# Reordered loads, a four-bank second layer for block 0 and moved weight sums in a retention and feed-forward kernel

## The chip, the core and the metric

The kernel runs on one core of one Trainium2 chip. The metric is the device time of one execution, in microseconds (us). Five engines matter, each with an instruction queue of its own that is worked off in order: PE (TensorE, the matrix multiplications), DVE (VectorE), ACT (ScalarE), POOL (GpSimd) and SP (SyncE, which here only issues DMA transfers). Matmul results land in PSUM, which holds eight banks of 128 x 512 fp32; everything else lives in SBUF.

## The reference

For each of 8 batches and 8 heads, 576 tokens of 64 dimensions go through retention (attention without a softmax, with a decay per head); the result, 4608 tokens of 512 values, goes through a two-layer network with GELU.

```python
scores = scale * q @ k.T                         # per batch and head
ret = scores * Dmat                              # Dmat[i, j] = gamma_h ** (i - j) for i >= j, else 0
x = (ret @ v) -> (4608, 512)                     # heads side by side
h = x @ w_in                                     # 512 -> 2048
out = (0.5 * h * (1 + tanh(c * (h + 0.044715 * h**3)))) @ w_out   # 2048 -> 512
```

All inputs and the output are fp32; the kernel computes in fp16 with fp32 sums.

## The kernel before, in words

**Blocks.** The network works on nine blocks of 512 tokens, t = 0 to 8. Block t below 8 holds the first 512 tokens of batch t; block 8 holds the last 64 tokens of all batches. While PE computes block t, the retention of batch t + 1 is woven in between. Batch 1 is thus prepared during block 0, batch 2 during block 1.

**Retention of batches 0 to 2.** The 512 tokens go in two groups g of 256 tokens. A group's inputs are six load tiles of 128 x 512 fp32 (256 KB): two each of q, k and v (`load`, L91). Each is cast to fp16 (`cast`, L244), q and k with a decay factor. Then, in this order: `turn` (L275) transposes q and k on PE, eight 128 x 128 transposes into one bank `tr`, and one engine copies them to `tt` in SBUF; `state2` (L341) multiplies k by v into two banks `us`; `score2` (L313) makes the scores in banks `st`, two for each half x; `masks2` (L327) multiplies them by the causal mask into `ret` on DVE and frees the bank; `scan` (L405, DVE) carries the decayed state on and frees `us`, and `spread` (L419, ACT) writes it as fp16; `past` and `av2` (L425, L356) make the output `xs`, and `put` (L455, ACT) copies that to `xT`.

**The network.** First layer: `up_half` (L480) does eight matmuls of 256 columns into a bank `hp` for half a block, and ACT applies GELU from `hp` into `gT`. Second layer of block 0: `down_mm` (L504), plain matmuls of 512 columns into a bank `op[i]` for each of four groups of 128 tokens, summed over 16 tiles of w_out; `store_pair` (L509) copies two banks to `ost` and stores them. Second layer of blocks 1 to 8: a seven-product scheme (`prod`, `after`, L548 and L568) in place of eight products. It needs sums of quarters of w_out, `wt` 1 to 4 (`weight_sums`, L525: four DVE instructions of 128 x 1024 fp16 for half of the rows; the call with f = 4 needs the last eight w_out tiles of the order below), and sums of quarters of gT (`act_sums`, L536: four DVE instructions).

**Loads.** `seq` (L124 to L131) lists all load tiles in the order in which SP issues them: batch 0, the 16 w_in tiles, the 16 w_out tiles in the order FO (L125), then batch by batch. They go through a ring of LD = 16 buffers; `pump` (L134) issues the next load when a cast has freed a buffer. w_out tiles are cast by POOL and DVE in turn (`cast_w`, L622, and WENG, L634).

**Order of the work.** The order on each engine is written out by hand. Each block is a list of PE steps, its *units* (L839 on); `at(t, u, f)` (L703) puts the work f behind unit u of block t. Block 0 has here 16 units of first layer before unit 0 (numbered -16 to -1) and 34 units of second layer (L842): for the banks op[0] and op[1] 16 units of two `down_mm` each and a store, then the same for op[2] and op[3]. Block 1 has 16 units of `up_half` (0 to 15) and 14 of `prod`, two for each product (products 1, 6, 5, 7, 2, 4, 3 at units 16 to 29). `group` (L718) places the two transposes, a first part (state, scores, masks) and a second part (past, av, put) of a group, `casts2` (L746) its casts. "(0, 17)" below is unit 17 of block 0.

PSUM banks are handed out in the order in which they were given back (`bank`, `drop`, L61 and L67): a matmul into a new bank waits until the bank's last reader is done.

Of the kernel before, what the change touches and what calls it, by code (L numbers as in the profile page):

```python
# [20 lines left out]
def kernel(  # L21
# [97 lines left out]
    def body(b):  # L119
        if b < NPE:  # L120
            return [("b", b, key, 2 * g + y) for g in range(2) for key in "qkv" for y in range(2)]
        return [("b", b, key, c) for c in range(NC) for key in "kqv"]

    seq = body(0) + [("i", g, ct) for g in range(4) for ct in range(4)]  # L124
    FO = [f + g for f in (0, 4) for g in (0, 1, 2, 3, 8, 9, 10, 11)]  # L125
    seq += [("o", f) for f in FO]
    TP = {2: 0, 4: 2, 6: 4, 7: 6}
    for b in range(1, B):
        seq += body(b)
        if b - 1 in TP:  # L130
            seq.append(("t", TP[b - 1]))  # L131
    q_ld = {"next": 0, "free": LD, "hold": False}
# [96 lines left out]
    def new_casts(b):  # L229
        a = att[b]  # L230
        for key in "kqv":
            a[key] = sb.tile([128, W], F16, tag="c" + key, name="c" + key, bufs=1 if key == "q" else 2)
# [38 lines left out]
    def new_turned(b):  # L271
        att[b]["tt"] = t = sb.tile([128, 2, NB, 128], F16, tag="tt", name="tt", bufs=2)
        att[b]["tk"], att[b]["tq"] = t[:, 0], t[:, 1]

    def turn(b, g, key, copies):  # L275
        a = att[b]
        n = HP // len(copies)
        src = a[key][:, 1024 * g : 1024 * g + 1024].rearrange("p (i j x) -> p i j x", j=2, x=2 * D)
        dst = a["tt"][:, "kq".index(key), 8 * g : 8 * g + 8, :]
        for x, cp in enumerate(copies):  # L280
            full = bank("tr", F16)
            t = full[:, 0 : 256 * n].rearrange("p (i j t) -> p i j t", j=2, t=128)
            for i in range(n):
                for j in range(2):
                    nc.tensor.transpose(t[:, i, j], src[:, n * x + i, j], ident)  # L285
            o = dst[:, 2 * n * x : 2 * n * x + 2 * n]
            if key == "q":
                o = o.rearrange("p (i h) (t j) -> p i j (h t)", h=2, j=2)
            else:
                o = o.rearrange("p (i j) t -> p i j t", j=2)  # L290
            cp(out=o, in_=t)
            drop(full)
# [20 lines left out]
    def score2(b, g, xs=(0, 1)):  # L313
        a = att[b]
        for x in xs:
            st = [bank("st") for _ in range(2)]
            for p in (2 * x, 2 * x + 1):
                for j in range(2):
                    o = 256 * (p % 2) + 128 * j
                    for h, hl in TILES:  # L320
                        nc.tensor.matmul(
                            st[hl][hv(h), o : o + 128], a["tt"][hv(hl), 0, 8 * g + 2 * p + j, hv(h)],
                            tq(b, 2 * g + h, p)[hv(hl)], start=True, stop=True,
                        )
            a["st", g, x] = st

    def masks2(b, g, x):  # L327
        for hl, t in enumerate(att[b].pop(("st", g, x))):
            r = sb.tile([128, 512], F16, tag="ret", name="ret", bufs=6)
            nc.vector.tensor_tensor(  # L330
                out=r.rearrange("p (n i) -> p n i", n=2), in0=t.rearrange("p (n i) -> p n i", n=2),
                in1=pm.rearrange("p j i -> p (j i)").unsqueeze(1).to_broadcast([128, 2, 256]), op=ALU.mult,
            )
            drop(t)
            att[b]["ret"][g, hl, x] = r
# [83 lines left out]
    def spread(b, c, cp):  # L419
        w = att[b].pop(("w", c))  # L420
        for hl in range(2):
            r = slice(64 * hl, 64 * hl + 64)
            cp(out=(tbd[b % 2][r, c, :, r] if c < NC - 1 else tbt[b % NT4][r, :, r]), in_=w[r])  # L423
# [98 lines left out]
    W11, W12 = w_out_sb[:, 0:NH, 0:HD], w_out_sb[:, 0:NH, HD:DM]  # L522
    W21, W22 = w_out_sb[:, NH:NF, 0:HD], w_out_sb[:, NH:NF, HD:DM]

    def weight_sums(f, ns=range(4)):  # L525
        s = slice(f, f + 4)
        for n in ns:
            o, x, y, f = (
                ("1", W12, W11, ALU.subtract), ("3", W22, W12, ALU.subtract),
                ("2", wt["3"], W11, ALU.add), ("4", W21, wt["2"], ALU.subtract),  # L530
            )[n]
            nc.vector.tensor_tensor(out=wt[o][:, s], in0=x[:, s], in1=y[:, s], op=f)  # L532

    gs = {}

# [86 lines left out]
    def cast_w(kind, *i):  # L622
        src = w_raw.pop((kind,) + i)
        if kind == "i":
            g, ct = i
            dst = w_in_sb[:, ct, 512 * g : 512 * g + 512]
        else:
            dst = w_out_sb[:, i[0], :]
        eng = WENG[kind][CP[kind] % len(WENG[kind])]
        CP[kind] += 1  # L630
        eng(out=dst, in_=src)  # L631
        pump(1)
# [13 lines left out]
    def later(b, c):  # L646
        scan(b, c)
        spread(b, c, A.copy)
# [54 lines left out]
    def at(t, u, f, last=False):  # L703
        events.setdefault((t, u, last), []).append(f)
# [5 lines left out]

    at(0, -12, lambda: [V.memset(x, 0.0) for x in (tbd[1][:, 1:], *tbt[1:])])
    for n, f in enumerate(FO):
        at(0, -5 + n // 4, lambda f=f: cast_w("o", f))
        if n > 8 and n % 2:
            at(0, -5 + n // 4, lambda n=n: weight_sums(0, [(n - 9) // 2]))


    def group(b, g, turns, s, o, own=True, ahead=()):  # L718
        for w, key, cp in zip(turns, "qk", (A.copy if b == 1 else T, A.copy)):
            at(*w, lambda key=key, cp=cp: turn(b, g, key, (cp,)))  # L720

        def first():
            if own:
                state2(b, g)
            score2(b, g)
            if own:
                later(b, 2 * g)
            masks2(b, g, 0)
            if own:
                masks2(b, g, 1)  # L730
                scan(b, 2 * g + 1)
            else:
                at(s[0], s[1] + 1, lambda: masks2(b, g, 1))

        def second():
            past(b, 2 * g), past(b, 2 * g + 1), av2(b, g)
            for x in ahead:
                state2(*x)
            put(b, 2 * g), put(b, 2 * g + 1)

        at(*s, first)
        at(*o, second)
        if own:
            at(o[0], o[1] + 1, lambda: spread(b, 2 * g + 1, A.copy))

    def casts2(b, g, kq, v, e):  # L746
        at(*kq, lambda: [cc(b, key, 2 * g + y, P) for key in "qk" for y in range(2)])
        at(*v, lambda: [cc(b, "v", 2 * g + y, e) for y in range(2)])

    at(0, 6, lambda: (new_casts(1), new_turned(1)))  # L750
    casts2(1, 0, (0, 7), (0, 21), A)
    group(1, 0, ((0, 17), (0, 20)), (0, 23), (0, 30))
    casts2(1, 1, (0, 14), (0, 29), A)
    at(0, 28, lambda: weight_sums(4))
    group(1, 1, ((0, 27), (0, 31)), (1, 1), (1, 6))
    at(1, 0, lambda: (new_casts(2), new_turned(2)))
    casts2(2, 0, (1, 0), (1, 0), P)
    group(2, 0, ((1, 4), (1, 7)), (1, 11), (1, 16), ahead=((2, 1),))
    casts2(2, 1, (1, 4), (1, 4), P)
    at(1, 17, lambda: later(2, 2))  # L760
    at(1, 23, lambda: later(2, 3))
    group(2, 1, ((1, 10), (1, 13)), (1, 20), (1, 26), own=False)
    at(1, 8, chunk_masks)

    at(6, 0, lambda: load_tails(TP[7]))
    at(6, 18, lambda: cast_tails(TP[7]))
# [72 lines left out]
    for t in range(NTB):  # L839
        steps = []  # L840
        if t == 0:
            for i0 in (0, 2):  # L842
                for f in FO:
                    steps.append(lambda f=f, i0=i0: [down_mm(0, i0 + n, f) for n in range(2)] and None)
                steps.append(lambda i0=i0: store_pair(0, i0, (A.copy, V.tensor_copy)))
        else:
            for u in range(2 if t == 1 else 0):
                for f in (0, NH, 2, NH + 2, 4, NH + 4, 6, NH + 6):
                    def half(u=u, f=f):
                        up_half(t, u, f)  # L850
                        if f in (NH + 2, NH + 6):
                            return lambda: act_sums(t, f - NH - 2, f - NH + 2, slice(u, u + 1))
                    steps.append(half)
            for f in range(0 if t == 1 else NH):
                steps.append(lambda f=f: up(t, f))
                def hi(f=f):
                    up(t, f + NH)
                    if f % 2:
                        return lambda: act_sums(t, f - 1, f + 1)
                steps.append(hi)  # L860
            for m in (1, 6, 5, 7, 2, 3, 4) if t == NTB - 1 else (1, 6, 5, 7, 2, 4, 3):
                for u in range(2):
                    steps.append(lambda m=m, u=u: (prod(t, m, u), after(t, m, u)))
        for u, s in enumerate(steps):
            then = s()
            run(t, u)
            if callable(then):
                then()
            run(t, u, True)
# [31 lines left out]
```

## Time and profile before

| | us |
|---|---|
| median of 3 runs | 300.15 (298.98 to 300.69) |
| the profiled execution, whole | 300.83 |
| its span (first to last instruction) | 298.9 |
| PE busy in the span | 284.7 |
| PE busy in 0 to 34 us | 27.41 of 34.00 |
| PE busy in 34 to 58 us | 20.99 of 24.00 |
| PE busy in 58 to 290 us | 232.00 of 232.00 |
| PE busy in 290 us to the end | 4.32 of 8.90 |

The last four rows are busy times of PE in stretches of the span. Second-layer matmuls of block 0 begin at 33.86 us, first-layer matmuls of block 1 at 53.99 us, products of block 1 at 74.04 us. "Busy" of PE runs to the modelled end of a matmul. An idle time is put down to the instruction or transfer that released it last.

### The profile page before, as it was taken

The numbers are of one execution on the slowest core, as the hardware profiler recorded it, in microseconds if no ns is written. First come the engines' busy times: TensorE is split into PE (matmuls) and PEld (weight loads), VectorE is DVE, ScalarE is ACT, GpSimd is POOL, SyncE is SP. The second block draws the span as 40 slices with busy tenths as digits, with TensorE's granted clock in tenths as the row PEclk, the third lists the DMA queues.
The fourth block names the chain that finished last, engine by engine and source line by source line (L and its number), as shares of the span: only waits on it lengthen the run. The fifth ranks groups of instructions, "written<-read, shape, count | busy, mean of one in ns | idle before, by whom it ended". The sixth has DMA issues, their size and how long they took to land.

```text
span 298.9 us, 7301 instructions
## 1 busy us (share of the span) xinstructions
PE 284.7 (95%) x3028; PEld 197.2 (66%) x3028; DVE 171.9 (58%) x353; ACT 163.4 (55%) x302; POOL 98.8 (33%) x129
## 2 busy tenths in 40 slices
PE   6779988899999999999999999999999999999993
PEld 2458645688884488448844885488548854884582
DVE  6790445998754874476548654855486535233432
ACT  5377426788438673766376736664665356307500
POOL 4677377970790074006700650058030000000000
PEclk9999999999999999999999999999999999999998
DMA  7999999999889999999999959944931030012004
GB/s 200 309 352 350 371 271 293 246 289 211 178 147 230 227 217 183 268 207 195 118 245 227 181 99 263 219 90 86 255 86 37 2 140 0 2 50 94 0 0 140
DMA packets 129057, 52.89 MB, mean 177 GB/s; under 512 B 101633, under 2 KB 120577, under 8 KB 129025
## 3 DMA queue, kind: packets, MB, share of 16 engines
q1 hardware_dynamic: 128544, 51.92, 73.7%
q10 hardware_dynamic: 480, 0.52, 0.6%
q8 instruction: 23, 0.38, 0.5%
q14 instruction: 10, 0.07, 0.1%
HBM read 36.70 MB, written 9.44 MB: 154 GB/s over the span
## 4 chain that ended last, share of the span: by engine, by line
PE 80%; DMA 10%; DVE 4%; SPq 3%; POOL 2%; ACT 1%; issue 0%; DVEq 0%; POOLq 0%
PE hp L469 33%; PE opB L561 14%; PE opA L561 10%; PE opC L561 10%; PE hp L487 4%; DMA ld<-in_moe_w_out_dram 4%; SPq L96 2%; PE xs L448 2%; PE st L372 2%; DMA ld<-in_moe_w_in_dram 2%; DMA ld<-in_q_dram 2%; DMA ld<-in_v_dram 2%; DVE wt L532 2%; PE xs L439 1%; PE us L397 1%; PE tr L285 1%
## 5 line engine op out<-in xcount | busy, mean ns | idle before, releaser
L469 PE MATMUL hp<-xT,w_in_sb 128*128 128x512 f16 x448 | 98.9, 380 | 0.0
L475 ACT ACTIVATE gT<-hp 128x512 f16<-128x512 f32 x112 | 64.9, 597 | 45.3 <-PE hp L469 44.8
L469 PEld LDWEIGHTS <-w_in_sb 128*128 128x128 f16 x448 | 43.3, 98 | 50.6
L561 PEld LDWEIGHTS <-gT 128*128 128x128 f16 x512 | 49.0, 98 | 7.1 <-issue 0.7
L561 PEld LDWEIGHTS <-s 128*128 128x128 f16 x384 | 37.0, 98 | 4.9
L543 DVE TENSOR_TENSOR s<-gT 128x512 f16<-128x512 f16 x32 | 14.0, 436 | 44.4 <-ACT gT L475 44.4
L827 POOL COPY gate<-s 128x1 f16<-128x1 f16 x5 | 0.9, 189 | 92.3 <-DVE s L546 92.3
L561 PE MATMUL opB<-wt,gT 128*128 128x256 f16 x256 | 30.9, 273 | 0.5 <-DVE ost L575 0.5
L487 PE MATMUL hp<-xT,w_in_sb 128*128 128x256 f16 x256 | 30.2, 273 | 1.1 <-POOL w_in_sb L631 1.0
L561 PE MATMUL opA<-w_out_sb,gT 128*128 128x256 f16 x256 | 30.8, 273 | 0.0
L487 PEld LDWEIGHTS <-w_in_sb 128*128 128x128 f16 x256 | 24.4, 98 | 5.1 <-POOL w_in_sb L631 1.6
L423 ACT CAST tbd<-ws 64x256 f16<-64x256 f32 x48 | 19.3, 403 | 15.3 <-DVE ws L414 13.6
L381 DVE TENSOR_TENSOR ret<-st,cm 128x512 f16<-128x512 f32 x40 | 24.8, 681 | 0.0
L575 DVE TENSOR_TENSOR k<-k,opB 128x512 f32<-128x512 f32 x16 | 11.0, 687 | 22.2 <-PE opB L561 16.3
L605 ACT COPY ost<-opA 128x512 f32<-128x512 f32 x8 | 4.7, 586 | 34.2 <-PE opA L561 19.9
L264 POOL TENSOR_TENSOR cq<-ld,sc 128x512 f16<-128x512 f32 x20 | 21.9, 1095 | 0.0
L493 ACT ACTIVATE gT<-hp 128x512 f16<-128x512 f32 x32 | 18.5, 600 | 5.3 <-PE hp L487 5.0
L458 ACT CAST xT<-xs 128x512 f16<-128x512 f32 x36 | 19.3, 592 | 3.3 <-PE xs L362 1.9
L264 POOL TENSOR_TENSOR ck<-ld,sc 128x512 f16<-128x512 f32 x20 | 20.8, 1040 | 0.0
L414 DVE TENSOR_TENSOR ws<-vs,gt 128x256 f32<-128x256 f32 x24 | 16.0, 669 | 1.2
L575 DVE TENSOR_TENSOR ost<-k,opC 128x512 f32<-128x512 f32 x16 | 11.0, 687 | 9.8 <-PE opC L561 9.5
L575 DVE TENSOR_TENSOR ost<-k,opB 128x512 f32<-128x512 f32 (+1 forms) x9 | 5.7, 629 | 18.7 <-PE opB L561 18.7
(93 smaller groups left out, 359.1 us busy)
## 6 DMA issues: line engine op xcount, KB each, us to landing
ld<-in_q_dram SPq DMA_DIRECT2D x32, 256.0 KB, 5.4
ld<-in_k_dram SPq DMA_DIRECT2D x32, 256.0 KB, 5.3
ld<-in_v_dram SPq DMA_DIRECT2D x32, 256.0 KB, 5.3
out_dram<-ost SPq DMA_DIRECT2D x16, 512.0 KB, 3.5
ld<-in_moe_w_in_dram SPq DMA_DIRECT2D x16, 256.0 KB, 6.2
ld<-in_moe_w_out_dram SPq DMA_DIRECT2D x16, 256.0 KB, 6.1
lt<-in_k_dram SPq DMA_DIRECT2D x8, 128.0 KB, 5.1
lt<-in_q_dram SPq DMA_DIRECT2D x8, 128.0 KB, 4.4
```

The lines of the kernel that those rows point to most:

```text
L264: eng.tensor_tensor(out=dst.rearrange("p (h d) -> p h d", d=D), in0=raw.rearrange("p (h d) -> p h d", d=D), in1=sc[:, s0].unsqueeze(2).to_ ...
L381: nc.vector.tensor_tensor(out=r.rearrange("p (n i) -> p n i", i=128), in0=t.rearrange("p (n i) -> p n i", i=128), in1=(cm if b < PAIR else ...
L414: nc.vector.tensor_tensor(out=w, in0=uc, in1=gt, op=ALU.mult)
L423: cp(out=(tbd[b % 2][r, c, :, r] if c < NC - 1 else tbt[b % NT4][r, :, r]), in_=w[r])
L458: nc.scalar.copy(out=xT[:, g0 : g0 + 2], in_=xs.rearrange("p (n g t) -> p g n t", n=HP, g=2))
L469: nc.tensor.matmul(hp.rearrange("p (g t) -> p g t", t=TL), w_in_sb[:, ct, 128 * fc : 128 * fc + 128], xT[:, o : o + TB // TL, ct, :], star ...
L475: nc.scalar.activation(out=gT[t][:, fc].rearrange("p i n -> p (i n)"), in_=hp, func=AF.Gelu_apprx_tanh)
L487: nc.tensor.matmul(hp[:, 256 * x : 256 * x + 256].rearrange("p (g t) -> p g t", t=TL), w_in_sb[:, ct, 128 * (f + x) : 128 * (f + x) + 128] ...
L493: nc.scalar.activation(out=gT[t][:, f : f + 2, 2 * u : 2 * u + 2, :].rearrange("p f i n -> p f (i n)"), in_=hp.rearrange("p (f n) -> p f n ...
L543: nc.vector.tensor_tensor(out=s["1"], in0=a21, in1=a22, op=ALU.add)
L561: nc.tensor.matmul(op[tag][:, HD * u : HD * u + HD], lhs(f), rhs[:, f], start=(new and u == 0 and f == 0), stop=(f == NH - 1), skip_group_ ...
L575: nc.vector.tensor_tensor(out=o, in0=a, in1=b, op=ALU.add)
```

## The change

Six edits:

1. `seq` lists the first six tiles of batch 1 (group 0: q, k, v) behind the twelfth w_out tile; the last four w_out tiles follow, then the rest of batch 1.
2. Block 0's second layer runs in two turns over all four banks: the first twelve w_out tiles for op[0] and op[1] (units 0 to 11), then for op[2] and op[3] (12 to 23), then the last four tiles for each pair (24 to 27, store at 28; 29 to 32, store at 33). Four banks are held from unit 12 on.
3. The last four w_out tiles are cast by POOL alone, behind unit 6. The first four weight sums (f = 0) move to unit -3; the other four (f = 4), which lay together at (0, 28), go in pairs to (1, 9) and (1, 12).
4. With four banks held, group 0 of batch 1 takes its scores in two halves of two banks each, units 20 and 24 (`apart=4`). Its spread of the second state goes to (1, 1).
5. The casts, transposes and parts of batch 1 and 2 move: casts of q and k of batch 1 from units 7 and 14 to 2 and 14, v from ACT at units 21 and 29 to ACT at 18 and POOL at 15; transposes of group 0 from units 17 and 20 to 13 and 17, of group 1 from 27 and 31 to 31 and (1, 0); the first part of group 0 from unit 23 to 20, that of group 1 stays at (1, 1). In batch 2 some events move by one unit. The chunk masks go from (1, 8) to (1, 14).
6. The transposed q of batch 2 is copied by ACT in place of DVE; of the second store of block 0, both copies are on DVE.

```diff
@@ load order @@
-    seq += [("o", f) for f in FO]
+    LATE = 12
+    seq += [("o", f) for f in FO[:LATE]]
     TP = {2: 0, 4: 2, 6: 4, 7: 6}
+    seq += body(1)[:6] + [("o", f) for f in FO[LATE:]] + body(1)[6:]
     for b in range(1, B):
-        seq += body(b)
+        seq += body(b) if b > 1 else []
@@ cast_w @@
-        eng = WENG[kind][CP[kind] % len(WENG[kind])]
+        eng = WENG[kind][CP[kind] % len(WENG[kind])] if CP[kind] < LATE or kind == "i" else nc.gpsimd.tensor_copy
@@ events @@
     for n, f in enumerate(FO):
-        at(0, -5 + n // 4, lambda f=f: cast_w("o", f))
-        if n > 8 and n % 2:
-            at(0, -5 + n // 4, lambda n=n: weight_sums(0, [(n - 9) // 2]))
+        at(0, -5 + n // 4 if n < LATE else 6, lambda f=f: cast_w("o", f))
+        if 8 <= n < LATE:
+            at(0, -5 + n // 4, lambda n=n: weight_sums(0, [n - 8], V))
@@ group @@
-        for w, key, cp in zip(turns, "qk", (A.copy if b == 1 else T, A.copy)):
-            at(*w, lambda key=key, cp=cp: turn(b, g, key, (cp,)))
+        for w, key in zip(turns, "qk"):
+            at(*w, lambda key=key: turn(b, g, key, (A.copy,)))
 ...
-            score2(b, g)
+            score2(b, g, (0,) if apart else (0, 1))
             if own:
                 later(b, 2 * g)
             masks2(b, g, 0)
+            if own and not apart:
+                masks2(b, g, 1)
             if own:
-                masks2(b, g, 1)
                 scan(b, 2 * g + 1)
-            else:
+            if apart:
+                at(s[0], s[1] + apart, lambda: (score2(b, g, (1,)), masks2(b, g, 1)))
+            elif not own:
                 at(s[0], s[1] + 1, lambda: masks2(b, g, 1))
@@ placing @@
-    at(0, 6, lambda: (new_casts(1), new_turned(1)))
-    casts2(1, 0, (0, 7), (0, 21), A)
-    group(1, 0, ((0, 17), (0, 20)), (0, 23), (0, 30))
-    casts2(1, 1, (0, 14), (0, 29), A)
-    at(0, 28, lambda: weight_sums(4))
-    group(1, 1, ((0, 27), (0, 31)), (1, 1), (1, 6))
+    at(0, -1, lambda: (new_casts(1), new_turned(1)))
+    casts2(1, 0, (0, 2), (0, 18), A)
+    group(1, 0, ((0, 13), (0, 17)), (0, 20), (0, 29), apart=4, late=(1, 1))
+    casts2(1, 1, (0, 14), (0, 15), P)
+    group(1, 1, ((0, 31), (1, 0)), (1, 1), (1, 5), late=(1, 6))
     at(1, 0, lambda: (new_casts(2), new_turned(2)))
     casts2(2, 0, (1, 0), (1, 0), P)
-    group(2, 0, ((1, 4), (1, 7)), (1, 11), (1, 16), ahead=((2, 1),))
+    group(2, 0, ((1, 4), (1, 6)), (1, 10), (1, 15), ahead=((2, 1),))
     casts2(2, 1, (1, 4), (1, 4), P)
-    at(1, 17, lambda: later(2, 2))
+    at(1, 9, lambda: weight_sums(4, (1, 2), V))
+    at(1, 12, lambda: weight_sums(4, (0, 3), V))
+    at(1, 16, lambda: later(2, 2))
     at(1, 23, lambda: later(2, 3))
-    group(2, 1, ((1, 10), (1, 13)), (1, 20), (1, 26), own=False)
-    at(1, 8, chunk_masks)
+    group(2, 1, ((1, 9), (1, 12)), (1, 20), (1, 26), own=False)
+    at(1, 14, chunk_masks)
@@ units of block 0 @@
-            for i0 in (0, 2):
-                for f in FO:
+            for i0, fs in ((0, FO[:LATE]), (2, FO[:LATE]), (0, FO[LATE:]), (2, FO[LATE:])):
+                for f in fs:
                     steps.append(lambda f=f, i0=i0: [down_mm(0, i0 + n, f) for n in range(2)] and None)
-                steps.append(lambda i0=i0: store_pair(0, i0, (A.copy, V.tensor_copy)))
+                if fs[-1] == FO[-1]:
+                    steps.append(lambda i0=i0: store_pair(0, i0, (V.tensor_copy if i0 else A.copy, V.tensor_copy)))
```

More of the change, by code (lines that the diff above doesn't have):

```diff
@@ L523, with weight_sums @@
     W21, W22 = w_out_sb[:, NH:NF, 0:HD], w_out_sb[:, NH:NF, HD:DM]
-    def weight_sums(f, ns=range(4)):
+    def weight_sums(f, ns, eng):
         s = slice(f, f + 4)
@@ L531, in weight_sums @@
             )[n]
-            nc.vector.tensor_tensor(out=wt[o][:, s], in0=x[:, s], in1=y[:, s], op=f)
+            eng.tensor_tensor(out=wt[o][:, s], in0=x[:, s], in1=y[:, s], op=f)
     gs = {}
@@ L712, with group @@
     for n, f in enumerate(FO):
-        at(0, -5 + n // 4, lambda f=f: cast_w("o", f))
-        if n > 8 and n % 2:
-            at(0, -5 + n // 4, lambda n=n: weight_sums(0, [(n - 9) // 2]))
-    def group(b, g, turns, s, o, own=True, ahead=()):
-        for w, key, cp in zip(turns, "qk", (A.copy if b == 1 else T, A.copy)):
-            at(*w, lambda key=key, cp=cp: turn(b, g, key, (cp,)))
+        at(0, -5 + n // 4 if n < LATE else 6, lambda f=f: cast_w("o", f))
+        if 8 <= n < LATE:
+            at(0, -5 + n // 4, lambda n=n: weight_sums(0, [n - 8], V))
+    def group(b, g, turns, s, o, own=True, ahead=(), apart=0, late=None):
+        for w, key in zip(turns, "qk"):
+            at(*w, lambda key=key: turn(b, g, key, (A.copy,)))
         def first():
@@ L743, in group @@
         if own:
-            at(o[0], o[1] + 1, lambda: spread(b, 2 * g + 1, A.copy))
+            at(*(late or (o[0], o[1] + 1)), lambda: spread(b, 2 * g + 1, A.copy))
     def casts2(b, g, kq, v, e):
```

## The prediction

> **What bounds the kernel now.** I read the page's busy shares first, then PE's busy time by stretches, then what PE waited for, then the chain of waits in the stretch with gaps.
>
> The page: span, shares, and PE's row of the 40 slices (tenths busy, 7.5 us each).
>
> ```profile
> span 298.9 us, 7301 instructions
> PE 284.7 (95%) x3028; PEld 197.2 (66%) x3028; DVE 171.9 (58%) x353; ACT 163.4 (55%) x302; POOL 98.8 (33%) x129
> PE   6779988899999999999999999999999999999993
> ```
>
> PE is the bound, and its gaps lie in the start, in slices 5 to 8 and at the end. The change touches nothing ahead of 33 us and nothing of the last block. It adds and removes no PE instruction: both programs have 6058 PE rows in the order of instructions. So it can only gain PE's gaps between 34 us and the point from which PE is full; the table of stretches above has 232.00 of 232.00 us busy from 58 to 290 us. The stretches between (us, busy us and instructions of PE, PEld, DVE, ACT, POOL, then clock, DMA share, GB/s):
>
> ```profile
> 34.00:54.00 20.00, 18.07 (x198) 9.34 (x196) 11.23 (x19) 8.93 (x14) 13.77 (x15) 1.00 1.04 291
> 54.00:74.00 20.00, 18.93 (x328) 16.56 (x328) 18.53 (x31) 15.54 (x29) 11.03 (x15) 1.00 1.00 249
> ```
>
> The prize is 1.93 + 1.07 = 3.00 us, 1.0% of the time, and no more. PE's waits from 33.8 to 60 us (total, times, longest):
>
> ```profile
> PE st L321 <- DVE ost L513: 1.1, 1, 1.1
> PE tr L285 <- POOL cq L256: 1.0, 1, 1.0
> PE us L348 <- ACT cv L251: 0.8, 2, 0.4
> ```
>
> Three gaps, then: 1.02 us until batch 1's q is cast (in PE's timeline the transposes at 42.39 us), 0.78 us until its v is cast (0.45 and 0.33, at 46.76 and 47.28 us), 1.07 us until a bank is free for scores (57.62 us). 0.13 us is in crumbs. Why they arise stands in the chain of waits (start, duration):
>
> ```profile
> 34.63 5.48 DMA ld<-in_q_dram
> ...
> 40.28 2.05 POOL cq L256 x2
> 42.33 2.02 POOL ck L256 x2
> ...
> 52.00 2.07 DVE wt L532 x2
> ...
> 54.09 1.43 DVE wt L532
> ...
> 55.54 1.42 DVE wt L532
> 56.96 0.61 DVE ost L513
> ...
> 57.62 0.41 PE st L321 x15
> ```
>
> Gap one is the transfer: q is issued behind 16 w_out tiles and lands at 40.1 us. Gap three is the four weight sums at (0, 28): 5.0 us on DVE with the copy that frees the op bank queued behind them.
>
> **Part 1, the earlier loads (edit 1).** The transfers run back to back, so order decides. DVE's timeline starts the cast of the twelfth w_out tile at 36.57 us, on its landing. In the casts that wait for w_out a tile takes 0.67 us (DVE at 28.57, POOL at 29.27, DVE at 29.91); from q's landing at 40.1 to the third q tile, whose cast starts at 45.20, six tiles pass, 0.84 each. So batch 1's first tile lands at 36.55 + 0.85 = 37.4, the four q and k tiles by 39.9, v by 41.6, the late w_out tiles at 42.3 to 44.3, and the third q tile at 45.15 as before, since the bytes ahead of it are the same. POOL has just finished its sixth w_out cast (35.95, 0.79 us) and casts q and k in 4 x 1.02: q ready at 39.5, k at 41.5.
>
> PE's side: a unit is 0.435 us (eight matmuls from 48.10 to 49.84). From 33.86, unit 13 ends at 39.95, the q transposes take 0.45 (42.39 to 42.84), unit 17 ends at 42.1, the k transposes at 42.6, unit 20 at 43.9. q is 0.45 us ahead of its use, k 0.6. **Gap one goes: -1.02**, and with it the crumbs, -0.13. The late w_out tiles, cast by POOL (0.61 to 0.8 each) by 45.0, are wanted at unit 24, about 47 us. Those casts stand ahead of group 1's q, k and v casts in POOL's queue, but these wait for the transfers of 45.15 us and later anyway, and their transposes only come at unit 31, near 51. On SP the six loads pass four w_out issues; the two stores of block 0 now stand behind batch 3's first loads, and no engine waits for a store. Cover gone: each us by which q or k casts slip beyond 0.5 is a us of PE.
>
> **Part 2, v (edit 5).** Between the k transposes and `state2` there are three units in both kernels, and ACT does the same there: copy of k (1.01 us), two v casts. Before, state2 ran 1.91 and 2.43 us after the transposes ended (44.85 to 46.76 and 47.28). **Gap two stays: 0** (bounds: -0.78 if ACT is quicker, +0.3 if q's copy of 1.31 delays k's).
>
> **Part 3, four banks in two turns (edits 2 and 4).** The matmuls are the same. With four op banks held, state2 and the first scores take the other four. The second scores, four units (1.74 us) later, need the first freed `us` and `st`: 0.34 + 0.6 us of DVE work, so over 0.5 us spare. Cost 0 (bounds 0 to +0.6, one mask of 0.68 late).
>
> **Part 4, the weight sums off (0, 28) (edit 3).** The op copies then meet an idle DVE. Both copies of the second store are done within 1.3 us (0.61 each) of unit 32's end; the scores of (1, 1) come two `up_half` units (2 x 0.87), the k transposes and state2 later. **Gap three goes: -1.07.** What is late next: group 1's k is now transposed at (1, 0), and PE has only 0.87 + 0.28 us until the scores. ACT needs the GELU of (1, 0) out of the way (0.25 us past the transposes), then 1.01 for the copy and 0.05: 1.31 against 1.15. **New wait: +0.15** (bounds 0 and +0.6).
>
> **Part 5, the sums in block 1.** DVE is the tight engine there: 18.53 of 20 us from 54 to 74. In exchange for four sums it loses two copies of batch 2's q (1.30 and 1.31, at 64.72 and 68.50 us). A sum took 0.68 alone and 1.42 beside POOL:
>
> ```profile
> 35.59 0.68 DVE L532 TENSOR_TENSOR wt<-w_out_sb 128x1024 f16<-128x1024 f16 x1
> 54.09 1.42 DVE L532 TENSOR_TENSOR wt<-wt,w_out_sb 128x1024 f16<-128x1024 f16 x1
> ```
>
> Unit (1, 9) falls at about 65 us (66.97 less 2). POOL's batch 2 casts start when group 1's q is transposed, about 51.6, and take 8 x 1.02 + 4 x 0.6 = 10.6 us alone, 13.1 with the stretching seen before: done at 62 to 64.7. So I price the sums at 4 x 0.68 = 2.72 against 2.61 lost. First user: product 7 (bank opB, at 81.14 us in the old time) waits for the add that empties the bank. Before, that add ended at 79.68. Now the spread of batch 2's third state (at (1, 16) instead of (1, 17)) stands ahead of ACT's copy L591 that the add needs: `ws` ends at 77.96, then 0.82 + 0.58 + 0.69 and hops make 80.2; with DVE's 0.1 more and a start 0.3 later against PE, 80.5. Spare 0.6. Cost 0 (bounds 0 and +4.2, second rival).
>
> The Trainium skill, SBUF — State Buffer, section "Who interferes with whom", says that a DVE instruction with two SBUF inputs and a GpSimd instruction that reads SBUF exclude each other, the later one blocked to the end of the earlier. The rows of 0.68 and 1.42 agree. By that rule four sums beside POOL would each wait up to one cast, 4 x 1.02 = 4.1 us, and past the spare the forecast would end 3.5 us later.
>
> **Part 6, copies on ACT (edit 6).** ACT has 15.54 us of work from 54 to 74; it gains 2 x 1.31 (the q copies at 43.04 us are on ACT: 1.31) and loses one op copy of 0.59: 17.6 in 18.9 us. PE waits for ACT only when hp banks run out. Cost 0 (bounds 0 and +1.3, one such copy ahead of a GELU).
>
> The Trainium skill, Perfetto Trace Analysis, section "Optimizing Scalar/DVE Operations", says that DVE is faster where it has a performance mode; that speaks against edit 6. Here the copies took 1.30 on DVE and 1.31 on ACT, so no cost comes from that; with a DVE copy at half its time the move would cost ACT the same 2.62 and leave DVE 1.3 less relief.
>
> **Sum.** -1.02 - 0.13 - 1.07 + 0.15 = -2.07 us. The profiled execution took 300.83 (span 298.9 and 1.93 around it), so it would take 298.76. It was 0.68 above the median of 300.15; from the median: **298.1 us**.
>
> **The rivals.**
> - *ACT takes over in block 1* (chance 0.22). For: 93% full, and each waiting GELU holds an hp bank. Against: 58 to 90 us has 18.69 of 31.8 on ACT, so it catches up in the products. It would return about 1.3: 299.4.
> - *DVE and POOL collide in block 1*, slower (0.10). If POOL's batch 2 casts run past 66 us, the sums cost 1.53 (the longest of the sums) instead of 0.68, +3.4, and a set of act_sums (0.83 and 0.71 beside POOL against 0.42) +1.4. Less the spare of 0.6: 4.2 on PE at product 7, net +2.1: 302.3. It decides from 0.6 us of lateness on, and undoes the gain at 2.7. Against: POOL's own sum above.
> - *The tiles do not come earlier* (0.08). Transfers have hiccups: the cast at 33.89 came 1.3 us late. If q is ready at 42.3 as now, PE waits 2.4 at unit 13 instead of 1.02: -2.07 + 2.4 = +0.3, 300.5.
>
> **How the numbers follow.** The forecast has 0.60. Runs spread from 298.98 to 300.69, so it covers 297.2 to 299.0. A range of 297.0 to 300.6 takes in the forecast, the first and third rival, and leaves out the second and a little below. 0.5%, 1.5 us, is about what a measurement can tell from no change. Faster (below 298.65): 0.48 of the forecast, 0.05 of the first rival: 0.53. Slower: 0.09. Same: 0.38.
>
> **What would show it.** q transposes at about 40 us without a wait; v's wait of 0.8 still there at 44 to 45 us; the four ost copies clear of any sum and no wait of `st` for DVE ost; sums of 0.68 near 66 and 73 us; PE idle from 34 to 74 us at 0.9 instead of 3.0. It is wrong if PE waits in block 1 for hp, tt or opB by over 0.5 us, or if q lands after 39 us.

## The result, and the profile after

The changed kernel takes 298.49 us (median of 20 runs, 298.0 to 300.06); the kernel before takes 300.2 us in the runs beside it (298.98 to 301.37). The ratio is 0.9946 with a 95% interval of 0.9932 to 0.996: 1.6 us faster, between 1.2 and 2.0. The forecast was 298.1 us. The profiled execution took 298.35 us, 2.48 less than that of before, where the sum had 2.07 less.

In the lists below, lines of the changed kernel stand two higher than in the kernel before (its L323 is the L321 of before).

The page of the changed kernel: span, shares, PE's row of 40 slices.

```profile
span 296.6 us, 7304 instructions
PE 285.3 (96%) x3028; PEld 197.6 (67%) x3028; DVE 168.5 (57%) x350; ACT 163.9 (55%) x301; POOL 100.1 (34%) x133
PE   6779999999999999999999999999999999999993
```

The three eights of slices 6 to 8 have become nines, and nothing else in PE's row has moved. The stretches of the changed kernel, with the columns as in the prediction (PE, PEld, DVE, ACT, POOL, clock, DMA share, GB/s):

```profile
34.00:54.00 20.00, 19.22 (x211) 10.83 (x209) 7.88 (x14) 8.66 (x13) 15.34 (x18) 1.00 1.14 303
54.00:74.00 20.00, 19.96 (x397) 17.68 (x396) 17.98 (x33) 18.47 (x34) 9.99 (x15) 1.00 1.04 246
```

PE idles 0.78 + 0.04 = 0.82 us in the two stretches, where it was 3.00. In the first row DVE has less to do (7.88 against 11.23), as the first two of the f = 4 weight sums, 2.1 us, stood there before, among other things. In the second ACT is now fuller than DVE (18.47 us, where ACT had 15.54 before). PE's waits of the changed kernel from 33 to 100 us (total, times, longest):

```profile
PE us L350 <- ACT cv L253: 0.8, 2, 0.4
```

Of three waits the one for v is left. PE's timeline of the changed kernel (start, duration; in brackets what it waited, and for what) shows it, and the places where the other two were:

```profile
39.63 0.61 PE L287 MATMUL tr<-ident,cq 128*128 128x128 f16 x8
...
44.15 0.19 PE L350 MATMUL us<-cv,ck 64*64 64x64 f16 x1 [0.45 <-ACT cv L253]
...
44.67 0.44 PE L350 MATMUL us<-cv,ck 64*64 64x64 f16 x31 [0.33 <-ACT cv L253]
...
54.12 0.44 PE L350 MATMUL us<-cv,ck 64*64 64x64 f16 x32
54.52 0.64 PE L323 MATMUL st<-tt 64*64 64x128 f16 x32
...
78.55 1.91 PE L563 MATMUL opB<-wt,gT 128*128 128x256 f16 x16
```

The transposes of q at 39.63 and the scores at 54.52 have no bracket. The two waits for v are those of before to the digit.

One thing got worse. Product 6 begins at 74.19 and product 7 at 78.55: 4.36 us, where 4.17 lay between them before (76.97 to 81.14). The 2.48 us of the profiled execution are made up so: the second layer of block 0 began 0.28 us earlier (33.58 for 33.86; in the 14 profiles of this case that start lies between 33.38 and 35.64, so this is scatter); from there to product 6 PE took 2.50 less; product 7 gave 0.19 back; 0.42 more was lost later, 0.3 of it in a wait in block 5 that no other profile has; the end and the time around the span were 0.31 shorter. Of the 2.50, 2.18 is idle time that went; the rest lies in modelled busy time, in which a short wait can hide (see e4).

DVE's timeline of the changed kernel (start, duration, line, what is computed) shows what the sums and their neighbours took in block 1:

```profile
59.29 1.27 DVE L545 TENSOR_TENSOR s<-gT 128x512 f16<-128x512 f16 x1
60.59 1.15 DVE L546 TENSOR_TENSOR s<-s,gT 128x512 f16<-128x512 f16 x1
61.67 0.83 DVE L547 TENSOR_TENSOR gT<-gT 128x512 f16<-128x512 f16 x1
62.42 0.82 DVE L548 TENSOR_TENSOR s<-gT,s 128x512 f16<-128x512 f16 x1
...
65.72 0.69 DVE L534 TENSOR_TENSOR wt<-w_out_sb 128x1024 f16<-128x1024 f16 x1
...
72.03 0.68 DVE L534 TENSOR_TENSOR wt<-w_out_sb 128x1024 f16<-128x1024 f16 x1
...
77.81 0.69 DVE L577 TENSOR_TENSOR k<-k,opB 128x512 f32<-128x512 f32 x1 [1.49 <-ACT k L593]
```

The weight sums took 0.68 to 0.69, as forecast. The four `act_sums` instructions ahead of them took 4.07 together. The same set in DVE's timeline of the kernel before took 2.45:

```profile
62.45 0.83 DVE L543 TENSOR_TENSOR s<-gT 128x512 f16<-128x512 f16 x1
63.32 0.71 DVE L544 TENSOR_TENSOR s<-s,gT 128x512 f16<-128x512 f16 x1
63.95 0.41 DVE L545 TENSOR_TENSOR gT<-gT 128x512 f16<-128x512 f16 x1
64.29 0.50 DVE L546 TENSOR_TENSOR s<-gT,s 128x512 f16<-128x512 f16 x1
```

The add that empties opB (L577) ended at 78.50, and product 7 began 0.05 us behind it.

### The profile page after: what moved, and what is told of

Its sections match the earlier page's. It is cut to its first block, busy times and chain, and to the rows that moved or that the text cites. A ratio compares the mean times of both kernels' runs of the same rounds, so it can differ in the third digit from the quotient of the medians.

```text
span 296.6 us, 7304 instructions
## 1 busy us (share of the span) xinstructions
PE 285.3 (96%) x3028; PEld 197.6 (67%) x3028; DVE 168.5 (57%) x350; ACT 163.9 (55%) x301; POOL 100.1 (34%) x133
## 4 chain that ended last, share of the span: by engine, by line
PE 89%; DVE 4%; ACT 3%; DMA 1%; issue 1%; POOL 0%; SPq 0%; ACTq 0%; POOLq 0%; DVEq 0%
PE hp L471 30%; PE opB L563 14%; PE opA L563 10%; PE opC L563 10%; PE hp L489 9%; PE op L509 4%; PE xs L450 2%; PE tr L287 2%; PE st L374 2%; PE xs L441 2%; ACT gT L477 1%; PE xs L364 1%; DMA ld<-in_q_dram 1%; ACT tbd L425 1%; PE st L323 1%; PE us L399 1%
## 5 line engine op out<-in xcount | busy, mean ns | idle before, releaser
L425 ACT CAST tbd<-ws 64x256 f16<-64x256 f32 x48 | 19.3, 403 | 16.3 <-DVE ws L416 15.7
L577 DVE TENSOR_TENSOR k<-k,opB 128x512 f32<-128x512 f32 x16 | 11.0, 687 | 22.2 <-PE opB L563 14.7
L293 ACT COPY tt<-tr 128x1024 f16<-128x1024 f16 (+1 forms) x12 | 11.8, 998 | 11.2 <-PE tr L287 11.1
L577 DVE TENSOR_TENSOR ost<-k,opC 128x512 f32<-128x512 f32 x16 | 11.0, 688 | 9.8 <-PE opC L563 9.5
L577 DVE TENSOR_TENSOR ost<-k,opB 128x512 f32<-128x512 f32 (+1 forms) x9 | 5.7, 628 | 18.8 <-PE opB L563 18.8
```

Source lines behind the costliest of these rows:

```text
L577: nc.vector.tensor_tensor(out=o, in0=a, in1=b, op=ALU.add)
```

## The experiments

**Theory:** the early tiles close gap one, the moved sums close gap three, v's gap stays, and the copies of batch 2's q on ACT pay for the sums in block 1. **Rivals:** the early tiles alone, with four banks, would have closed gap three too, or gap one is worth nothing in time; the sums collide with POOL in block 1.

In the table, "before" is the kernel before on the same chip. "PE stretch" is from the start of the first matmul of block 0's second layer to the start of the last matmul into opB: a measure of PE's path that leaves start and end out. "Waits" are PE's, from 33 to 92 us.

| kernel | median, us | before | ratio (95%) | PE stretch | waits |
|---|---|---|---|---|---|
| before | | | | 260.70 | q 1.0, v 0.8, scores 1.1 |
| changed | 298.49 | 300.2 | 0.9946 (0.9932 to 0.996) | 258.81 | v 0.8 |
| e1, sums alone | 298.33 | 300.17 | 0.992 (0.9892 to 0.9948) | 259.17 | q 0.7, v 0.8 |
| e2, sums at (0, 28) | 298.39 | 300.17 | 0.9934 (0.9906 to 0.9962) | 258.26 | v 0.8 |
| e3, loads back | 299.34 | 300.17 | 0.9973 (0.9949 to 0.9996) | 260.03 | q 1.5, v 0.8 |
| e4, v on DVE | 296.95 | 300.17 | 0.9884 (0.985 to 0.9918) | 257.34 | none |
| e5, sums beside POOL | 298.35 | 299.87 | 0.9949 (0.9925 to 0.9973) | 258.20 | v 0.8 |
| e6, q copies on DVE | 300.16 | 299.87 | 1.0004 (0.9977 to 1.0031) | 260.21 | hp 1.9, v 0.8 |
| e8, e1 with v on DVE | 297.47 | 299.87 | 0.9912 (0.9881 to 0.9942) | 257.02 | none |
| e9, e2 with v on DVE | 298.05 | 299.87 | 0.9923 (0.9896 to 0.995) | 258.31 | scores 0.2 |
| e10, changed again | 298.32 | 300.72 | 0.9932 (0.9907 to 0.9956) | 258.38 | v 0.8 |
| e11, e1 again | 298.2 | 300.72 | 0.9932 (0.9906 to 0.9958) | 259.72 | q 1.2, v 0.8 |
| e12, e4 again | 297.01 | 300.72 | 0.9897 (0.9869 to 0.9925) | 257.34 | none |
| e7, e4 with a later spread | 296.95 | 300.72 | 0.9878 (0.9854 to 0.9902) | 257.26 | none |

### Which edit closes which gap

**e1: the kernel before with the sums moved alone** (and, to make room for them on DVE, batch 2's q copied by ACT).

```diff
-    at(0, 28, lambda: weight_sums(4))
+    at(1, 9, lambda: weight_sums(4, (1, 2)))
+    at(1, 12, lambda: weight_sums(4, (0, 3)))
-        for w, key, cp in zip(turns, "qk", (A.copy if b == 1 else T, A.copy)):
+        for w, key, cp in zip(turns, "qk", (A.copy, A.copy)):
```

> The kernel before with one part of the change: the four weight sums of (0, 28) go to (1, 9) and (1, 12), and ACT copies batch 2's transposed q in place of DVE. Loads, the second layer of block 0 and batch 1 stay as they were. Theory (three separate gaps of PE): the scores at (1, 1) no longer wait 1.07 us for the bank, the waits for q (1.02) and v (0.78) stay, and DVE's load in block 1 is level (2.72 more, 2.61 less): 1.07 less than before, 299.1. Rival A (the early loads carry the whole gain, the sums' place is hidden behind another wait): 300.2. Rival B (DVE in block 1 has no room without the earlier start): a new wait for opB at product 7, 301 or more.

PE's waits of e1 from 33 to 100 us:

```profile
PE us L348 <- ACT cv L251: 0.8, 2, 0.4
PE tr L285 <- POOL cq L256: 0.7, 1, 0.7
```

The wait of the scores is gone without early tiles and without four banks: moving the sums is enough for gap three. The PE stretch is 1.53 shorter, 0.35 of it because the wait for q happened to be 0.67 instead of 1.02 in this profile. The time is as low as that of the changed kernel, and 0.8 below the 299.1 expected.

**e2: the changed kernel with the sums back at (0, 28).**

```diff
-    at(1, 9, lambda: weight_sums(4, (1, 2), V))
-    at(1, 12, lambda: weight_sums(4, (0, 3), V))
+    at(0, 28, lambda: weight_sums(4, range(4), V))
```

> The changed kernel with the four weight sums back together at (0, 28), all else as changed. Theory (the sums at (0, 28) make the wait for the bank): the op copies of the second store queue behind the sums again, the scores at (1, 1) wait about 1.1: 299.6 against 298.5 of the changed kernel. Rival: in the new order POOL is idle there (48.9 to 51.7 us in the changed kernel's trace), so the sums take 0.68 each, end near 52.5, and the copies are done at 53.8, ahead of the scores at 54.5: no wait, and DVE in block 1 is 2.7 us freer: 298.4, or a little less.

The rival was right. DVE's timeline of e2 ("x2" is two instructions back to back, their time together):

```profile
50.63 1.28 DVE L534 TENSOR_TENSOR wt<-w_out_sb 128x1024 f16<-128x1024 f16 x2
51.94 0.69 DVE L534 TENSOR_TENSOR wt<-wt,w_out_sb 128x1024 f16<-128x1024 f16 x1
52.67 1.42 DVE L534 TENSOR_TENSOR wt<-w_out_sb,wt 128x1024 f16<-128x1024 f16 x1
54.02 1.27 DVE L515 COPY ost<-op 128x512 f32<-128x512 f32 x2
```

And POOL's of e2, in the same stretch:

```profile
48.57 1.36 POOL L255 CAST cv<-ld 128x512 f16<-128x512 f32 x2
...
52.24 2.76 POOL L258 TENSOR_TENSOR cq<-ld,sc 128x512 f16<-128x512 f32 x2 [2.30 <-PE tr L287]
```

POOL casts nothing from 49.93 to 52.24 us. Three of the four sums fall into that hole and take 0.67 to 0.69 each; only the fourth meets the next cast and takes 1.42. In the kernel before the four took 5.0 us in the same place. So gap three had two remedies, each enough: move the sums, or move POOL's work away from them.

The hole does not come from the early tiles. POOL's timeline of e3 (next), which has the old load order and all else as changed, has it too:

```profile
49.21 1.36 POOL L255 CAST cv<-ld 128x512 f16<-128x512 f32 x2
53.14 2.05 POOL L258 TENSOR_TENSOR cq<-ld,sc 128x512 f16<-128x512 f32 x2 [2.58 <-issue]
```

There is one buffer for the cast q, so batch 2's q casts wait until batch 1's second q is transposed: they begin 0.14 us after these transposes end (52.10 to 52.24 in e2; 51.56 to 51.70 in the changed kernel). Edit 5 moved those transposes from unit 27 to unit 31. By these rows that is what keeps POOL off the sums; no run moves the transposes alone.

**e3: the changed kernel with the loads in the old order** (four banks, places and casts as changed).

```diff
-    seq += [("o", f) for f in FO[:LATE]]
+    seq += [("o", f) for f in FO]
-    seq += body(1)[:6] + [("o", f) for f in FO[LATE:]] + body(1)[6:]
+    seq += body(1)
```

> The changed kernel with the load order of before: all 16 w_out tiles, then batch 1; units, banks and casts as changed. Theory (the order of the transfers decides when q is there): q lands four w_out tiles, 2.7 us, later, its second cast ends near 42 and the transposes behind unit 13, at 39.8, wait about 2.2: 300.7, a little over before. Rival (casts or the ring of buffers decide, not the order of the transfers): 298.5, no wait at unit 13.

PE's waits of e3 from 33 to 92 us:

```profile
PE tr L287 <- POOL cq L258: 1.5, 1, 1.5
PE us L350 <- ACT cv L253: 0.8, 2, 0.4
```

q landed at 38.79 us, and PE waited 1.47 for it at unit 13, less than expected as the transfers came sooner than in the profile of before (40.12). The PE stretch is 1.22 longer than the changed kernel's (1.65 longer than that of e10, which is the changed kernel again, without the odd wait in block 5); the median is 0.85 higher. In the trace the early tiles are needed once q's transposes stand at unit 13; in time the intervals of e3 and of the changed kernel overlap.

**e10 and e11: the changed kernel and e1 again, on one chip.** e10 has no edit, e11 that of e1.

> The changed kernel itself, on one chip with the three runs that follow, so that small differences can be read. 298.2 to 298.6.

> The same kernel as e1_sums_only, beside the changed one. Theory (the wait for q is a gap of its own, which only the early loads close): 0.7 to 1.0 more than e10_changed_again, the wait for q again in the trace. Rival (the gain of the early loads is given back in block 1 or later, by a wait for opB or for transfers): within 0.3 of e10_changed_again.

PE's waits of e11 from 33 to 92 us:

```profile
PE tr L285 <- POOL cq L256: 1.2, 1, 1.2
PE us L348 <- ACT cv L251: 0.8, 2, 0.4
```

In the profiles e11 has gap one (1.2) and a PE stretch 1.34 longer than e10's. In the times they are equal: ratio 0.9932 both, 298.2 and 298.32. The intervals are 0.005 wide, 1.5 us, so this does not show that gap one costs nothing, but there is no sign in the times of the 1.2 that the profile gives it. One observation may bear on it: the profiled execution of a kernel with the old load order is up to 2 us above that kernel's own median (before 0.6, e1 0.7, e8 1.3, e11 2.0; e3 0.0), that of one with early tiles 0.57 at most and about 0.1 on average. If the wait for q is shorter in the executions that are not profiled, both fit. The spans on record point the same way. The other five executions of e11 have spans of 296.2 to 296.8 us, the profiled one 298.4. With its PE stretch and end they would have begun the second layer at 32.2 to 32.8 us, earlier than any profile (33.38 at the least). The same sum for e10 gives 33.5 to 34.0, but for one execution of 298.5, which agrees with the profiles. So PE's path was probably shorter in those executions of e11; that it was the wait for q is argued, not shown.

### What the sums cost in block 1

**e5: the sums at (1, 2), in the middle of POOL's casts of batch 2.**

```diff
-    at(1, 9, lambda: weight_sums(4, (1, 2), V))
-    at(1, 12, lambda: weight_sums(4, (0, 3), V))
+    at(1, 2, lambda: weight_sums(4, range(4), V))
```

> The changed kernel with all four weight sums of f = 4 at (1, 2), where POOL casts batch 2 (51.7 to 63 us in the changed kernel's trace). The collision rival of the prediction: the sums take 1.42 instead of 0.68, 3.0 us more on DVE, 1.0 of it in an idle time; the add ahead of product 7 is 2 us late: 300.5. Theory now: the first set of act_sums, which takes 4.1 us beside POOL there (1.27, 1.15, 0.83, 0.82), is pushed behind POOL's casts and takes 1.7, so the two prices nearly cancel (+3.0 - 2.4 - 1.0): 298.4 to 298.8.

DVE's timeline of e5:

```profile
59.83 2.98 DVE L534 TENSOR_TENSOR wt<-w_out_sb 128x1024 f16<-128x1024 f16 x2
62.85 0.98 DVE L534 TENSOR_TENSOR wt<-wt,w_out_sb 128x1024 f16<-128x1024 f16 x1
63.87 0.98 DVE L534 TENSOR_TENSOR wt<-w_out_sb,wt 128x1024 f16<-128x1024 f16 x1
64.77 0.50 DVE L545 TENSOR_TENSOR s<-gT 128x512 f16<-128x512 f16 x1
```

The sums collide as the rival says: 4.94 us for four, against 2.7. But the `act_sums` set that had stood beside those casts now comes after them (its first instruction is the last line above) and takes 1.8 instead of 4.07. The one pays for the other, PE sees nothing (4.17 from product 6 to 7), and the time stays about as expected. The price of the rival counted only the instructions that move under POOL's casts, not those that move out from under them.

**e6: the copies of batch 2's transposed q on DVE again.**

```diff
-        for w, key in zip(turns, "qk"):
-            at(*w, lambda key=key: turn(b, g, key, (A.copy,)))
+        for w, key, cp in zip(turns, "qk", (A.copy if b == 1 else T, A.copy)):
+            at(*w, lambda key=key, cp=cp: turn(b, g, key, (cp,)))
```

> The changed kernel with the transposed q of batch 2 copied by DVE again (two copies of 1.30), as before. Theory (DVE has no room at product 7, where the add ends as PE wants the bank, and this edit pays for the moved sums): 2.6 us more on DVE, 1.0 of it in an idle time, 1.6 at the add: PE waits about 1.6 for opB: 300.1. Rival (ACT, 18.5 of 20 us busy from 54 to 74, is the tight one, and the chain to the add runs through ACT): 298.5 or less.

DVE's timeline of e6, the copy of the first q:

```profile
63.69 1.29 DVE L293 COPY tt<-tr 128x1024 f16<-128x1024 f16 x1
```

PE's timeline of e6, the matmuls that follow:

```profile
65.03 1.03 PE L489 MATMUL hp<-xT,w_in_sb 128*128 128x256 f16 x8 [1.11 <-DVE tt L293]
...
69.00 1.91 PE L489 MATMUL hp<-xT,w_in_sb 128*128 128x256 f16 x16 [0.79 <-DVE tt L293]
```

PE loses 1.11 + 0.79 = 1.9 us, and the time is that of before. The place was not the one expected. Banks are handed out in the order of return, so the first-layer matmul at 65.03 waits for the bank of a transpose, which DVE copies late. It is the wait for a bank of another stage that shows DVE's overload, well ahead of product 7. In the kernel before, with these copies on DVE and without the sums there, PE had no such wait.

### The gap that the change left

**e4: the changed kernel with v of batch 1's group 0 cast by DVE, at (0, 13).**

```diff
-    casts2(1, 0, (0, 2), (0, 18), A)
+    casts2(1, 0, (0, 2), (0, 13), V)
```

> The changed kernel with the two v casts of batch 1's first group on DVE at (0, 13) in place of ACT at (0, 18). DVE is idle from 36.2 to 45.2 us there, and v lands at 39.0 and 39.9. Theory (the wait left before state2, 0.45 + 0.33 us, comes only from ACT doing k's copy first): the wait goes, 0.8 less: 297.7. Rival (the scores behind state2 wait for k's copy on ACT, or the time is given back at product 7, where the add on DVE ends just as PE wants the bank): 298.2 to 298.5.

The stretch from 34 us in e4, columns as above:

```profile
34.00:54.00 20.00, 20.00 (x276) 11.41 (x273) 10.06 (x18) 8.55 (x12) 16.55 (x19) 1.00 1.13 303
```

PE has no idle time left in it. The casts began at 39.38 and 40.13 on DVE and took 0.43 and 0.86; the second was done at 40.99, 2.7 us ahead of its use at 43.72. The median is 1.5 us below the changed kernel's, the PE stretch 1.47: more than the 0.78 of the two waits, and more than expected.

The traces explain most of the difference. Of the 1.47, 0.43 lies behind product 7, where the changed kernel's profile has its odd loss; the other 1.03 lies ahead of product 6. There the two brackets say too little, as they count from the modelled end of the matmul before. From the first state product to the first scores PE takes 0.77 with the second wait (44.15 to 44.92) and 0.27 without it (43.72 to 43.99 in e4): that wait costs 0.50, not 0.33. With the 0.45 in front this makes 0.95.

**e8: e1 with the same cast, at (0, 17).**

```diff
-    casts2(1, 0, (0, 7), (0, 21), A)
+    casts2(1, 0, (0, 7), (0, 17), V)
```

> The kernel before with the sums moved as in e1_sums_only, and the v casts of batch 1's first group on DVE at (0, 17) instead of ACT at (0, 21). Loads and the second layer stay as before. Theory: of the three gaps only the wait for q (0.7 to 1.0) is left: 298.33 - 0.8 = 297.5; the early loads and the four banks are worth what is missing to 296.95 of e4_v_on_dve. Rival (with the late loads v itself lands too late, at 43.5 and 44.3, or the casts meet other DVE work): 298.3.

297.47 us as expected, 0.5 above e4 (on another chip), with no early tile and no four banks. The theory left the wait for q, but its profile shows no wait for q or v, though q landed as late as in e1 (39.74 and 39.76). Its second layer began late, at 35.64 instead of 33.86. The stretches of e8, columns as above, show why:

```profile
20.00:22.00 2.00, 2.00 (x42) 1.72 (x40) 1.56 (x5) 0.60 (x1) 1.92 (x4) 0.50 0.97 347
22.00:24.00 2.00, 2.00 (x26) 1.51 (x15) 0.00 (x0) 1.46 (x3) 1.86 (x4) 0.76 0.90 253
```

The granted clock of PE was 0.50 and 0.76 here and 0.89 in the 2 us before, where it was 1.00 in e1: 1.0 + 0.5 + 0.2 = 1.7 us of PE lost, estimated from these clocks. PE came so much later to q that q was cast 1.03 us ahead of its use. So gap one depends on how PE's start falls against the loads (0, 0.67, 1.02 and 1.21 in e8, e1, before and e11, all with the same load order and q transposed at unit 17), and this profile cannot price it. The early tiles with four banks thus differ by 0.5 us here and by -0.1 in e10 and e11, both within the intervals: the times do not tell their worth.

**e9: e2 with the same cast** (sums at (0, 28), v on DVE).

```diff
-    casts2(1, 0, (0, 2), (0, 18), A)
+    casts2(1, 0, (0, 2), (0, 13), V)
-    at(1, 9, lambda: weight_sums(4, (1, 2), V))
-    at(1, 12, lambda: weight_sums(4, (0, 3), V))
+    at(0, 28, lambda: weight_sums(4, range(4), V))
```

> The changed kernel with both the v casts on DVE (as e4_v_on_dve) and the four sums at (0, 28) (as e2_sums_at_28). Theory (the sums fit into DVE's idle time before the second op copies, and block 1 is rid of them, so the 0.1 to 0.2 wait for opB at product 7 goes too): 296.8. Rival (with PE 0.8 earlier the sums reach into POOL's casts and the op copies come late for the scores of (1, 1)): 297.2 or more.

PE's waits of e9 from 33 to 92 us:

```profile
PE st L323 <- DVE ost L515: 0.2, 1, 0.2
```

And from 86 to 290 us, in block 2:

```profile
PE st L374 <- DMA ett<-e: 0.5, 1, 0.5
```

The rival was right: the time is 1.25 above the 296.8 of the theory. PE and DVE run ahead of e2 here, and the sums begin at 49.18, beside POOL's v casts, and take 4.2 us, so the copies that free the bank are just late. A transfer in block 2 is the next that PE waits for; e4, e7 and e12, with their gaps closed too, have no such wait. With the sums in block 1 (e4) the PE stretch is 0.97 shorter.

**e12 and e7: e4 again, and e4 with the spread of batch 2's third state back at (1, 17).**

```diff
-    at(1, 16, lambda: later(2, 2))
+    at(1, 17, lambda: later(2, 2))
```

> The same kernel as e4_v_on_dve, beside the changed one. The closed wait for v is worth 0.8, and in the first set of runs it was 1.5. Theory: 0.8 less than e10_changed_again. Rival (something else is closed with it): 1.5 less.

> As e12_v_on_dve_again, and the scan and spread of batch 2's third state at (1, 17) as before the change, instead of (1, 16). Theory (at (1, 16) ACT's copy that the add ahead of product 7 needs is queued behind that spread, which costs PE 0.1 to 0.2 for opB): the add comes 1.5 us earlier, and 0.1 to 0.2 less than e12_v_on_dve_again. Rival (the wait is only moved to the next user): the same as e12_v_on_dve_again.

ACT's timeline of e12, the spread (L425) and the copy that the add ahead of product 7 needs (L593):

```profile
75.27 0.82 ACT L425 CAST tbd<-ws 64x256 f16<-64x256 f32 x2 [2.17 <-DVE ws L416]
76.11 0.59 ACT L593 COPY k<-opA 128x512 f32<-128x512 f32 x1
```

The same two in e7:

```profile
73.71 0.59 ACT L593 COPY k<-opA 128x512 f32<-128x512 f32 x1 [0.22 <-PE opA L563]
...
75.65 0.82 ACT L425 CAST tbd<-ws 64x256 f16<-64x256 f32 x2 [1.36 <-DVE ws L416]
```

In e12 the copy stands behind a spread that waits 2.17 us for DVE's `ws`. In e7 it goes first and is done 2.4 us sooner. The add moves from 76.73 to 75.54, and product 7 comes 4.17 us behind product 6 instead of 4.35. So the 0.19 at product 7 goes with the spread's place. It takes the sums at (1, 9) and (1, 12) as well: e2, e5 and e9 have the spread at (1, 16) and the sums elsewhere, and there product 7 also comes 4.17 behind product 6. In time, 0.18 us cannot be measured: 296.95 and 297.01. e12 against e10, on one chip, prices the wait for v: 1.31 us in the medians, 1.04 in the PE stretch. These are the fastest kernels of all, 3.2 to 3.8 us below the kernel before on their chip.

## Why the prediction was right, and where it was not

- **The bound.** Right. The gain is PE's idle time from 34 to 74 us: 3.00 became 0.82, forecast 0.9. That the change touches nothing ahead of 33 us holds for PE alone: SP issues the early q at 29.35 and DVE begins the first weight sum at 31.68 (35.59 before).
- **Part 1, gap one (-1.02).** Right in the trace: q landed at 35.55, 0.91 behind the twelfth w_out tile (forecast 0.85), and its transposes at 39.63 waited for nothing. The margin was not the one forecast. The transfers ran 1.9 us sooner than in the profile of before (the twelfth tile landed at 34.64, forecast 36.55), and q's second cast ended at 38.16, 1.47 ahead of its use instead of 0.45. In other profiles with these loads the margin lies between 0.27 (e9) and 2.02 (e6). In the time gap one is not confirmed: e11, which has it in its profile, is as fast as e10, which has not. What gap one is worth to an execution that is not profiled stays open.
- **Part 2, v (0).** Right to the digit: 0.45 and 0.33 are still there. e4 shows the cause (ACT's casts behind its copy of k) and that it was the cheapest thing left: one changed engine, 1.3 to 1.5 us in the medians, 1.04 of PE.
- **Part 3, four banks (0).** Right, no wait in block 0 for a bank.
- **Part 4, gap three (-1.07).** Right in size, and half right in cause. e1 shows that moving the sums is enough, e2 that it was not needed once POOL's casts of batch 2 began later (behind the q transposes of group 1, now at unit 31). The step took "5.0 us on DVE" as given in the old place; it was the sums' length beside POOL's casts, which Part 5 prices at 1.42 against 0.68 for one. The new wait of 0.15 was about 0.13: from the state products at 54.12 to the scores at 54.52 PE takes 0.40, where the same step in group 0 of batch 2 (65.52 to 65.79) takes 0.27. It shows no bracket.
- **Part 5, the sums in block 1 (0).** The sums' 0.68 was right; the spare of 0.6 at product 7 was none. The step took 0.1 us for DVE's extra lateness and did not count that the first `act_sums` set falls under POOL's casts (4.07, where it took 2.45). With the copy behind the spread, PE lost 0.19. The spread at (1, 17) (e7) undoes that, and so do the sums in other places (e2, e5, e9).
- **Part 6, q copies on ACT (0).** Right. ACT was busy 18.47 of 20 us, forecast 17.6 of 18.9, and PE never waited for it. e6 shows that this edit pays for the moved sums: without it 1.9 us go again. On the page that Part 6 names, its reading was one-sided: the Trainium skill, Perfetto Trace Analysis, section "Optimizing Scalar/DVE Operations", says in the same sentence that offloading some work to Scalar may make sense if DVE is saturated, and DVE had 18.53 of 20 us here.
- **The rivals.** ACT did not take over at 92% busy. The collision of DVE and POOL happened (4.07), but its price was wrong: e5 forces it on all four sums, and `act_sums` gets back what they lose. The tiles came earlier.
- **The size.** The measured gain, 1.6 us (1.2 to 2.0), is below the sum's 2.07 and below the profiled execution's 2.48. Of the 0.5 missing, 0.19 is Part 5's spare. The rest may be gap one, by e10 and e11, or the noise of the medians; no run here tells these apart. The forecast of 298.1 is close to the 298.49 measured, but of its three gaps only gap three is confirmed in the time (e1), and there the time gained more (1.8 us) than the trace's 1.07.

## What to carry to other kernels

Price a stretched row by what ran beside it before you move it: the four sums of 5.0 us were 2.7 us of work, and either they or their neighbour could move. Where an instruction leaves or enters another engine's casts, count who takes its place there. When several gaps follow one another, look also for the one that the change leaves (here v's): it cost one engine's name and gave nearly as much as all the rest. A wait for a transfer that one profile shows can be 0 or 1.2 us in the next (gap one): take several profiles before you price it.

## What the runs showed of the hardware

- DVE fp16 instructions with two SBUF inputs stretched beside POOL's casts: 128 x 512 took up to 1.27 us against 0.40 to 0.43 alone, 128 x 1024 up to 1.53 against 0.68. The masks with one PSUM input (`ret`) stayed at 0.6 in the same stretch. The Trainium skill, SBUF — State Buffer, section "Who interferes with whom", has DVE instructions with two SBUF inputs contend with GpSimd instructions that read SBUF; the rows agree. In e5 the price passed from one set to the other: the four sums took 2.2 us more, the four `act_sums` 2.3 less.
- With PE's gaps closed, one profile of four (e9) has PE wait for a transfer next, 0.5 us in block 2; e4, e7 and e12 have no wait there.
- The two waits for v, 0.78 us by their brackets, cost PE 1.04 us (PE stretch of e12 against e10). Idle time before a matmul is counted from a modelled end, and here it said too little.
- In e8 the granted clock of PE fell to 0.50 from 20 to 22 us and 0.76 from 22 to 24 us; its second layer began 1.8 us later than in e1. What lowered it was not traced.
